# Gated MLP on one core: the last 48 turns by Strassen's algorithm, partial sums added in DRAM by DMA

## The chip, the cores and the metric

One core of a Trainium2 chip runs the whole program. Its engines are TensorE (PE, with its weight loads as PEld), VectorE (DVE), ScalarE (ACT), GpSimd (POOL) and SyncE (SP), which issues the DMAs. A time is the device time of one execution in microseconds (us); the measure is the median of several runs.

## The reference, cut to what matters

```python
attn_out = _attn_ref(q, k, v, lam)            # linear attention with decay: (4, 8, 768, 64)
x = attn_out.transpose(0, 2, 1, 3).reshape(3072, 512)
x = _moe_ref(x, phi, w1, w2)                  # soft mixture of 8 experts, 32 slots: (3072, 512)

def _moe2_ref(x, w_in, w_out):                # the gated MLP: d_model 512, d_ff 2048
    h = x @ w_in
    g = h * (1.0 / (1.0 + np.exp(-1.702 * h)))
    return g @ w_out                          # out (3072, 512)
```

w_in and w_out come as 64-bit floats and are turned into 32-bit ones on the chip. The mixture ends as x = c @ slot_out with only 32 slots, so the kernel forms slot_out @ w_in once (`W2s`) and gets h as W2s times c. What remains large is g @ w_out: 3072 x 2048 x 512.

## The kernel before

Attention, slots and experts fill the first 195 us, and neither version differs there in what it computes. Then the gated MLP runs in **turns**. Tokens are cut into 4 groups `tg` of TG = 768, and d_ff into 16 blocks `f` of 128; a turn is one pair (tg, f), and `order` lists all 64.

A turn j does two things on TensorE. It makes h for turn j + 2 (`h_mm`, L940: two matmuls of 384 columns), and it adds block f into the output of its 768 tokens (`out_mm`, L987): for each of 6 token tiles of 128 rows, three matmuls of 512 columns, ghi x whi, ghi x wlo and glo x whi, since operands are split into a high and a low part of the type fp32r. The six sums stand in six PSUM banks `ob`. ScalarE applies the gelu (`h_gate`, L948) and rounds g to the high part (`h_hi`, L951); VectorE takes the low part as the difference (`h_lo`, L954).

The first three token groups are interleaved, so that the conversion of w_in and w_out (`conversion`, L185 to L195, VectorE; `convert_abs`, L176, ScalarE) can keep up. The tables `LATE_IN` and `LATE_OUT` say at which turn each piece is converted, `load_late` brings its 64-bit form into one of NST = 3 buffers `f64` on SP's queue, and `split_w` splits w_out into `whi` and `wlo`. A token group that is left half done has its sums copied to SBUF (`part`, L994) and added at its end (L998). The program is written in a fixed order by hand (`tc.manual_schedule()`): each engine executes its instructions in the order of the code, `do_out` places other work between the matmuls of a turn by their number (`at`, `extra`), and semaphores carry the dependences. PSUM has eight banks, named in `BANKS`.

The last two turns run together, and the very last token tile is done in two halves of 256 columns (`out_last`, L1015), so that the first half is stored under the second.

Of the kernel before, what the change touches and what calls it, by code (L numbers as in the profile page):

```python
# [17 lines left out]
def attention_moe_gelu_kernel(  # L18
# [32 lines left out]
    NE = 1  # L51
# [6 lines left out]
    NHG = 2  # L58

    LATE_IN = {1: (2, 4, 5, 6), 2: (7, 8, 9, 10), 3: (11, 12, 13, 14)}  # L60
    LATE_OUT = {4: 6, 5: 10, 6: 12, 7: 14}
# [101 lines left out]
    w_in_sb = {n: winp.tile([P, KD, 512], F32, name=f"w_in{n}") for n in range(NE)}  # L163

    def load_f64(key, src, pool, n, bufs):
        t = pool.tile([P, n, 2], U32, tag="f64", name="f64", bufs=bufs)
        SP.dma_start(out=t.rearrange("p n t -> p (n t)"), in_=src)
        staged[key] = t
# [306 lines left out]
    with tc.manual_schedule():  # L475
# [296 lines left out]
        def convert_early(f):  # L772
            convert_abs(("out", f))
            wo[f] = ex.tile([P, DM], F32, tag="wo", name="wo", bufs=3)
            return conversion(("out", f), wo[f], DVE)
# [12 lines left out]
        for e in range(E):  # L788
# [7 lines left out]
            if e == 4:  # L796

                slotc_cm.__exit__(None, None, None)
                slotb_cm.__exit__(None, None, None)
                ex_cm = tc.tile_pool(name="ex", bufs=1, side="left", reuse_waits="tile")  # L800
                ex = ex_cm.__enter__()
                whi, wlo = [ex.tile([P, DM], F32R, name="whi0")], [ex.tile([P, DM], F32R, name="wlo0")]
            if e == E - 2:
                split_c(E - 1)
# [4 lines left out]
        order = [(tg, f) for tg in range(NHG) for f in range(HF)] + [(NHG, f) for f in range(NF)]  # L809
        order += [(tg, f) for tg in range(NHG) for f in range(HF, NF)]  # L810
        order += [(tg, f) for tg in range(NHG + 1, NT // TG) for f in range(NF)]
        first_of = {f: min(order.index((tg, f)) for tg in range(NHG + 1)) for f in range(NF)}
# [12 lines left out]
        def load_late():  # L825
# [7 lines left out]
            load_f64(key, src, ex, DM, NST)  # L833
# [12 lines left out]
        soT = w2p.tile([P, KD, G, NS], F32, name="soT")  # L846
        W2s = w2p.tile([P, DFF], F32R, name="W2s")
        wp = [w2p.tile([P, 512], F32R, name=f"wp{j}") for j in range(2)]
        w2raw = w2p.tile([P, 512], F32, name="w2raw")
        isumr = tailp.tile([P, P], F32R, tag="xT", name="isumr", bufs=NHP + 1)  # L850
        POOL.tensor_copy(out=isumr, in_=isum4.rearrange("p g s -> p (g s)"))
        for n in w_late:
            w_in_sb[n] = w_in_sb[n - 2] if n > 1 else mp.tile([P, KD, 512], F32, name=f"w_in{n}")

        def convert_late(j, rounds=9):
            work = []
            for key in turns.get(j, ()):
                if key[0] == "out":
                    o = wo[key[1]] = ex.tile([P, DM], F32, tag="wo", name="wo", bufs=3)
# [31 lines left out]
        load_late()  # L891
# [40 lines left out]
        bh, g, ghi, glo = {}, {}, {}, {}  # L932

        def h_mm(j, us=(0, 1)):
# [8 lines left out]
            g[j] = mp.tile([P, TG], F32, tag="g", name="g", bufs=2)  # L943
            ghi[j] = mp.tile([P, TG], F32R, tag="ghi", name="ghi", bufs=3)
            glo[j] = mp.tile([P, TG], F32R, tag="glo", name="glo", bufs=3)
# [34 lines left out]
        def out_mm(j, t, i):  # L980
            tg, f = order[j]
            begin = j == 0 or order[j - 1] != (tg, f - 1)
            end = j == NJ - 1 or order[j + 1] != (tg, f + 1) or (t == NTT - 1 and j == NJ - LAST - 1)
# [7 lines left out]
            if f < NF - 1:  # L991

                part[tg, t] = mp.tile([P, DM], F32, tag=f"part{t}" if tg in (0, NTG - 1) else f"part{tg}_{t}", name="part")
                ACT.activation(out=part[tg, t], in_=ob[t], func=AF.Copy)  # L994
                return
            o = mp.tile([P, DM], F32, tag="o", name="o", bufs=3)
            if (tg, t) in part:
                DVE.tensor_tensor(out=o, in0=ob[t], in1=part[tg, t], op=ALU.add)  # L998
            elif t % 2 == 0:
# [4 lines left out]

        def out_last():

            t = NTT - 1
            r0 = (NTG - 1) * TG + t * P
            terms = [(jj, a[jj], w[order[jj][1]]) for jj in range(NJ - LAST, NJ)
                     for a, w in ((ghi, whi), (ghi, wlo), (glo, whi))]  # L1010
            o = mp.tile([P, DM], F32, tag="o", name="o", bufs=3)
            for u in range(2):
                b = bank(HB[u], "bo")
                for n, (jj, a, w) in enumerate(terms):
                    PE.matmul(b[:, :H2], a[:, t * P:(t + 1) * P], w[:, halves[u]], start=(n == 0), stop=(n == len(terms) - 1))  # L1015
                DVE.tensor_tensor(out=o[:, halves[u]], in0=b[:, :H2], in1=part[NTG - 1, t][:, halves[u]], op=ALU.add)
                SP.dma_start(out=out[r0:r0 + P, halves[u]], in_=o[:, halves[u]])

        def do_out(j, at):
# [4 lines left out]
            elif j == NJ - LAST:  # L1024

                seq = [(jj, t, i) for t in range(NTT - 1) for jj in range(j, NJ) for i in range(3)]
# [4 lines left out]
            if j == NJ - LAST:  # L1031
                out_last()
# [3 lines left out]
        def w2_rest():  # L1036
# [7 lines left out]
                 (11, 4): lambda: w2_a(2, "xt"), (12, 4): lambda: w2_b(2, "xt"), (12, 8): lambda: w2_c(2),  # L1044
                 (15, 4): lambda: w2_a(3, "xt"), (16, 4): lambda: w2_b(3, "xt"), (16, 8): lambda: w2_c(3)}

        NJ = NTG * NF
        AHEAD = 2
        LAST = 2
# [6 lines left out]
        by_turns(second)  # L1056
        h_mm(0)
# [7 lines left out]
        for j in range(NJ - LAST + 1):  # L1065
            at = {n: work for (jj, n), work in extra.items() if jj == j}
            if j > 0:
                at[9] = lambda: ahead(j + AHEAD)
                if j in (9, 12, 16):

                    at[9], at[12] = lambda: h_mm(j + AHEAD, (1,)), at[9]
            do_out(j, at)

# [34 lines left out]
```

## Time and profile before

| | |
|---|---|
| median of 3 runs | 495.46 us (495.11 to 495.68) |
| span of the profiled execution | 493.7 us |
| PE, PEld busy | 485.0 us (98%), 380.7 us (77%) |
| DVE, ACT, POOL busy | 276.1, 273.9, 62.4 us |
| output matmuls of L987 | 382 of each of three kinds, 449 us busy in sum |
| DMA, HBM | 69.28 MB read, 6.29 MB written |

The span goes from the first to the last instruction of the profiled execution; the run's own time has some 1.8 us around it (495.46 against 493.7). A matmul's listed duration holds its passage through the array, so matmuls overlap one another: what one costs is read from the distance of starts. Of other engines too the distance of starts can be shorter than the duration.

### The profile page before, as it was taken

To read this page: it belongs to the slowest core of one execution; us is meant where nothing else is said; L and a number is where in the kernel's file an instruction comes from. 1 tells how busy PE (TensorE), PEld (TensorE's weight loads), DVE (VectorE), ACT (ScalarE), POOL (GpSimd) and SP (SyncE) were. 2 spreads that over 40 slices of the span, in tenths; PEclk is the share of its full clock that TensorE was granted. 3 is DMA by queue.
4 is the path that set the end of the run, shared out by engine and by line. 5 is a ranking of instruction groups with operands and counts; after the bars stand their busy time and mean duration, and the time that the engine had idled before them with its cause. 6 is when DMAs were issued, how large, how long until landed. Compare 5 with 4: busy or idle time off the path is not lost.

```text
span 493.7 us, 9458 instructions
## 1 busy us (share of the span) xinstructions
PE 485.0 (98%) x3561; PEld 380.7 (77%) x3561; DVE 276.1 (56%) x616; ACT 273.9 (55%) x569; POOL 62.4 (13%) x109
## 2 busy tenths in 40 slices
PE   8999999999999999999999999999999999999997
PEld 5887877877876445787877888888888888888886
DVE  4867888988874114997999884312251223322112
ACT  5778677777853335786876755533443344334432
POOL 3544344442212000000000000000000000000000
PEclk9999999999999999999999999999999999999999
DMA  8999999999999996344344310300030001100003
GB/s 183 259 285 291 277 267 286 282 265 276 238 348 355 381 394 252 116 139 160 129 170 142 116 44 0 127 1 0 1 127 1 0 1 66 64 1 0 1 0 127
DMA packets 82860, 76.18 MB, mean 154 GB/s; under 512 B 54400, under 2 KB 62848, under 8 KB 82816
## 3 DMA queue, kind: packets, MB, share of 16 engines
q1 hardware_dynamic: 82672, 75.58, 49.1%
q8 instruction: 28, 0.46, 0.4%
q14 instruction: 16, 0.13, 0.1%
q10 hardware_dynamic: 144, 0.00, 0.0%
HBM read 69.28 MB, written 6.29 MB: 153 GB/s over the span
## 4 chain that ended last, share of the span: by engine, by line
PE 85%; DVE 6%; DMA 6%; ACT 1%; issue 1%; SPq 1%; DVEq 0%
PE bo L987 52%; PE bhh L940 4%; PE bs L293 4%; PE bacc L765 3%; PE bh L743 3%; PE bx L340 3%; DMA stage<-in_moe_w_in_dram 3%; PE bx L332 2%; PE bq L255 2%; PE bst L306 2%; PE bt L351 1%; DMA w<-in_moe_w_dram 1%; PE bk L257 1%; DVE AT L296 1%; DMA v<-in_v_dram 1%
## 5 line engine op out<-in xcount | busy, mean ns | idle before, releaser
L987 PE MATMUL bo<-whi,glo 128*128 128x512 f32 x382 | 149.9, 394 | 0.0
L987 PE MATMUL bo<-wlo,ghi 128*128 128x512 f32 x382 | 149.8, 393 | 0.1
L987 PE MATMUL bo<-whi,ghi 128*128 128x512 f32 x382 | 149.0, 392 | 0.1
L954 DVE TENSOR_TENSOR glo<-g,ghi 128x768 fp32r<-128x768 f32 x64 | 61.3, 957 | 134.6 <-ACT ghi L951 134.4
L948 ACT ACTIVATE g<-bhh 128x384 f32<-128x384 f32 x128 | 56.3, 489 | 125.7 <-PE bhh L940 122.7
L987 PEld LDWEIGHTS bo<-wlo,ghi 128*128 128x128 f32 x382 | 71.7, 188 | 16.6 <-issue 2.5
L987 PEld LDWEIGHTS bo<-whi,glo 128*128 128x128 f32 x382 | 71.7, 188 | 15.7 <-DVE glo L954 0.3
L987 PEld LDWEIGHTS bo<-whi,ghi 128*128 128x128 f32 x382 | 71.7, 188 | 14.3 <-DVE W2s L898 0.5
L951 ACT ACTIVATE ghi<-g 128x768 fp32r<-128x768 f32 (+1 forms) x65 | 54.3, 836 | 2.1
L274 POOL TENSOR_TENSOR qdT<-qT,qtab 128x384 f32<-128x384 f32 x32 | 32.1, 1002 | 39.5 <-PE bx L332 17.8
L293 PEld LDWEIGHTS bs<-qT,kT 64*128 64x128 f32 x384 | 26.5, 191 | 13.1 <-DVE zsum L453 4.2
L293 PE MATMUL bs<-qT,kT 64*128 64x128 f32 x384 | 33.3, 295 | 1.8 <-DVE AT L296 1.3
L296 DVE TENSOR_TENSOR AT<-bs,dec 128x384 f32<-128x384 f32 x64 | 32.5, 550 | 3.0 <-PE bs L293 2.2
L940 PE MATMUL bhh<-cT,W2s 128*128 128x384 f32 x128 | 33.4, 337 | 0.0
L265 ACT ACTIVATE qT<-bq 128x384 f32<-128x384 f32 x32 | 22.6, 705 | 16.4 <-PE bq L255 15.4
L940 PEld LDWEIGHTS bhh<-cT,W2s 128*128 128x128 f32 x128 | 23.9, 188 | 5.5
L281 ACT ACTIVATE kd<-k,dec 128x192 f32<-128x192 f32 x64 | 25.5, 447 | 2.9 <-DVE dec L497 1.3
L340 PE MATMUL bx<-AT,v 128*64 128x128 f32 x384 | 27.0, 273 | 0.0
L340 PEld LDWEIGHTS bx<-AT,v 128*64 128x64 f32 x384 | 21.0, 137 | 0.1
L332 PE MATMUL bx<-qdT,sa 128*128 128x128 f32 x128 | 19.8, 277 | 0.0
L317 DVE SCALAR_TENSOR_TENSOR sa<-sa,qtab,bst 64x64 f32<-64x64 f32 x64 | 17.9, 280 | 2.1
L306 PE MATMUL bst<-v,kd 128*64 128x64 f32 x320 | 17.6, 232 | 1.4 <-DMA v<-in_v_dram 1.2
(171 smaller groups left out, 597.9 us busy)
## 6 DMA issues: line engine op xcount, KB each, us to landing
w<-in_moe_w_dram SPq DMA_DIRECT2D x64, 512.0 KB, 6.3
f<-in_moe_w_out_dram SPq DMA_DIRECT2D x15, 512.0 KB, 3.2
qr<-in_q_dram SPq DMA_DIRECT2D x32, 192.0 KB, 4.2
k<-in_k_dram SPq DMA_DIRECT2D x64, 96.0 KB, 4.0
v<-in_v_dram SPq DMA_DIRECT2D x64, 96.0 KB, 4.0
f<-in_moe_w_in_dram SPq DMA_DIRECT2D x12, 512.0 KB, 4.1
out_dram<-o SPq DMA_DIRECT2D x23, 256.0 KB, 2.1
stage<-in_moe_w_in_dram SPq DMA_DIRECT2D x8, 256.0 KB, 4.1
```

Source lines behind the costliest of these rows:

```text
L274: POOL.tensor_tensor(out=qdT[s], in0=qT[s].rearrange("m (c i) -> m c i", c=R), in1=qtab[:, hp, None, :].to_broadcast([P, R, P]), op=ALU.mult)
L281: ACT.activation(out=t[:, :, h, :], in_=k_t[s][:, :, h, :], func=AF.Copy, scale=dec[:, 2 * hp + h, P - 1:P])
L293: PE.matmul(bs[h][:, cs], kT[s][hs, cs], qT[s][hs, cs], start=True, stop=True)
L296: DVE.tensor_tensor(out=t, in0=bs[h][:, :HS].rearrange("m (c i) -> m c i", c=R), in1=dec[:, 2 * hp + h, None, :].to_broadcast([P, R, P]), ...
L306: PE.matmul(bst[h * D:(h + 1) * D, c * D:(c + 1) * D], kd[s][:, c, h, :], v_t[s][:, c, h, :], start=True, stop=True)
L332: PE.matmul(bx[:, c * P:(c + 1) * P], state(s, first + c), qdT[s][:, c, :], start=(c == chunks[0]), stop=False)
L340: PE.matmul(bx[h * D:(h + 1) * D, c * P:(c + 1) * P], v_t[s][:, c, h, :], AT[s, h][:, c, :], start=False, stop=(c == R - 1))
L940: PE.matmul(bh[j][u][:, :HS], W2s[:, f * P:(f + 1) * P], cT[tg // (NTG // 2)][:, t0:t0 + HS], start=True, stop=True)
L948: ACT.activation(out=g[j][:, u * HS:(u + 1) * HS], in_=bh[j][u][:, :HS], func=AF.Gelu_apprx_sigmoid)
L951: ACT.activation(out=ghi[j][:, o], in_=g[j][:, o], func=AF.Copy)
L954: DVE.tensor_tensor(out=glo[j][:, o], in0=g[j][:, o], in1=ghi[j][:, o].bitcast(F32), op=ALU.subtract)
L987: PE.matmul(ob[t], a[j][:, t * P:(t + 1) * P], w[f], start=(begin and i == 0), stop=(end and i == 2))
```

## The change

The 64 turns become 32 as before and 48 of a new kind. The old kind now covers f = 0 to 3 of token groups 0 and 1, f = 0 to 7 of group 3, and all of group 2; the tables of conversions are spread to match, and the partial sums of groups 0, 1 and 3 are stored to `out` in DRAM instead of being kept in SBUF.

The rest (groups 0 and 1 from f = 4, group 3 from f = 8) is done in **groups** of 256 tokens (gi, nine of them; six turns in each of the first six, four in the last three). A new turn takes a pair p of blocks f = 2p, 2p + 1: a product of a 2 x 2 matrix of 128 x 128 blocks of g with a 2 x 2 matrix of 128 x 256 blocks of w_out. Strassen's algorithm (in Winograd's form) needs 7 block products instead of 8, each here three matmuls of 256 columns. For that it wants sums of blocks: four of w_out per pair (`make_sums`, `make_his`, `make_lows`, made once in the first half), and four of g per turn (in `s_h`, VectorE), with high and low parts of all seven (`s_hi`, ScalarE; `s_lo`, VectorE). h of turn j + 3 is made in turn j (`s_h`: two matmuls of 256). The sums of a group stand in 3 PSUM banks, alternating between two sets, and the first product in a shared one.

At a group's end `ev_m` (ScalarE) and `ev_a` to `ev_d` (VectorE) combine the seven sums to the four blocks of the output in `cells`, during the first three turns of the next group, and two DMAs on POOL's queue add them to `out` in DRAM. The last group is added on chip: its partial sums are loaded (`load_before`), and its last two turns run together (`last_turns`).

```diff
+    PAIR_AT = {2: 18, 3: 21, 4: 24, 5: 26, 6: 28, 7: 29}
+    LAST_HF = 8
...
+        WHOLE = 2
+        SPLIT = [tg for tg in range(NT // TG) if tg != WHOLE]
+        done = {tg: LAST_HF if tg == SPLIT[-1] else HF for tg in SPLIT}
+        order = [(tg, f) for tg in SPLIT for f in range(done[tg])] + [(WHOLE, f) for f in range(NF)]
...
-                part[tg, t] = mp.tile([P, DM], F32, tag=f"part{t}" if tg in (0, NTG - 1) else f"part{tg}_{t}", name="part")
-                ACT.activation(out=part[tg, t], in_=ob[t], func=AF.Copy)
+            o = mp.tile([P, DM], F32, tag="o", name="o", bufs=3)
+            if tg != WHOLE:
+                ACT.activation(out=o, in_=ob[t], func=AF.Copy)
+                SP.dma_start(out=out[r0:r0 + P, :], in_=o)
                 return
...
+            for o, x, y in ((b11, b12, b11), (b12, b22, b12), (b22, b22, b11), (b21, b21, b22)):
+                DVE.tensor_tensor(out=o, in0=x, in1=y, op=ALU.subtract)
...
+        PRODS = {1: (0, 1), 2: (2, 2), 3: (6, 3), 4: (1, 7), 5: (3, 4), 6: (4, 5), 7: (5, 6)}
+        PO = (2, 6, 7, 5, 3, 4, 1)
...
+        def s_h(j):
...
+            for k in range(2):
+                PE.matmul(b[:, k * NC:(k + 1) * NC], W2s[:, (2 * p + k) * P:(2 * p + k + 1) * P],
+                          cT[tg // 2][:, t0:t0 + NC], start=True, stop=True)
+            a = gs(j)
+            ACT.activation(out=a[:, :2 * NC], in_=b, func=AF.Gelu_apprx_sigmoid)
+            a21, a11, a22, a12, s1, s2, s3, s4 = (a[:, i * P:(i + 1) * P] for i in range(8))
+            for o, x, y, op in ((s1, a21, a22, ALU.add), (s3, a11, a21, ALU.subtract),
+                                (s2, s1, a11, ALU.subtract), (s4, a12, s2, ALU.subtract)):
+                DVE.tensor_tensor(out=o, in0=x, in1=y, op=op)
...
+            ACT.activation(out=sh[j], in_=gs(j)[:, P:], func=AF.Copy)
...
+            DVE.tensor_tensor(out=sl[j], in0=gs(j)[:, P:], in1=sh[j].bitcast(F32), op=ALU.subtract)
...
+            PE.matmul(bank_of(gi, i)[1], x, w, start=begin, stop=end)
...
+        def ev_a(gi):
+            DVE.tensor_tensor(out=cells[:, U2:C11 + 1:C11 - U2], in0=cells[:, M1:M1 + 1].to_broadcast([P, 2, H1]),
+                              in1=two(sbank[gi][0]), op=ALU.add)
...
+        def ev_out(gi):
+            for k in range(2):
+                POOL.dma_start(out=rows_of(gi, k), in_=cells[:, C11 + 2 * k:C11 + 2 * k + 2], accum_op=ALU.add)
...
+            at = {0: [lambda: s_hi(j + 2)], 9: [lambda: s_h(j + 3), lambda: s_lo(j + 2)]}
+            if gi and k < len(EV):
+                at[14] = [lambda: EV[k](gi - 1)]
...
+            s_turn((NSJ - 2, NSJ - 1), {2: [lambda: EV[2](gi - 1)], 6: [lambda: ev_m(gi)], 18: [first], 30: [second], 42: [lambda: ev_d(gi)]},
+                   (1, 2, 6, 7, 5, 3, 4))
```

On TensorE, in the second half before: a piece of a turn around its h pair (`bo` an output bank, `bhh` the bank of h, numbers those of a block of w_out).

```order
L987 MATMUL bo<-whi_3324,ghi 128x512
L987 MATMUL bo<-wlo_3339,ghi 128x512
L987 MATMUL bo<-whi_3324,glo 128x512
L940 MATMUL bhh<-cT,W2s 128x384 x2
L987 MATMUL bo<-whi_3324,ghi 128x512
```

In the change, the same place of a new turn (`bp` a group's bank, `tc` sums of w_out, `bsh` the bank of h, `GHI` and `GLO` the parts of g and its sums).

```order
L1166 MATMUL bp<-whi_3326,GHI 128x256
L1166 MATMUL bp<-wlo_3341,GHI 128x256
L1166 MATMUL bp<-whi_3326,GLO 128x256
L1166 MATMUL bp<-tc,GHI 128x256 x2
L1166 MATMUL bp<-tc,GLO 128x256
L1166 MATMUL bp<-tc,GHI 128x256 x2
L1166 MATMUL bp<-tc,GLO 128x256
L1122 MATMUL bsh<-cT,W2s 128x256 x2
L1166 MATMUL bp<-tc,GHI 128x256 x2
L1166 MATMUL bp<-tc,GLO 128x256
```

The 512-column products became runs of 256, three per block product, and a pair of 256 stands where the pair of 384 stood.

On VectorE, the end of the program before: one low part per turn, and the copies and adds of finished tiles.

```order
L998 TENSOR_TENSOR o<-bo,part 128x512 x3
L954 TENSOR_TENSOR glo<-g,ghi 128x768 x14
L1002 COPY o<-bo 128x512 x2
L1016 TENSOR_TENSOR o<-bo,part 128x256 x2
L1103 UNCONDITIONAL_BRANCH
```

In the change, VectorE in the first three turns of a later group (`f` is the buffer that `cells` lies in).

```order
L1176 TENSOR_TENSOR f_3197<-f_3197,bp 128x2x256
L1129 TENSOR_TENSOR G_all<-G_all 128x128 x4
L1141 TENSOR_TENSOR GLO<-G_all,GHI 128x896
L1180 TENSOR_TENSOR f_3197<-f_3197,bp 128x256
L1183 TENSOR_TENSOR f_3197<-f_3197,bp 128x2x256
L1129 TENSOR_TENSOR G_all<-G_all 128x128 x4
L1141 TENSOR_TENSOR GLO<-G_all,GHI 128x896
L1187 TENSOR_TENSOR f_3197<-f_3197,bp 128x512
```

Each turn now has four sums and a wider low part, and `ev_a` (L1176), `ev_b` and `ev_c` (L1180, L1183) and `ev_d` (L1187) stand behind the low parts, ahead of the next turn's sums.

In the change, VectorE at the end of the program: the eviction of the group before the last, then that of the last with the loaded partial sums (`before`).

```order
L1180 TENSOR_TENSOR f_3197<-f_3197,bp 128x256
L1183 TENSOR_TENSOR f_3197<-f_3197,bp 128x2x256
L1187 TENSOR_TENSOR f_3197<-f_3197,bp 128x512
L1176 TENSOR_TENSOR f_3197<-f_3197,bp 128x2x256
L1232 TENSOR_TENSOR f_3197<-f_3197,before 128x256 x2
L1180 TENSOR_TENSOR f_3197<-f_3197,bp 128x256
L1232 TENSOR_TENSOR f_3197<-f_3197,before 128x256
L1183 TENSOR_TENSOR f_3197<-f_3197,bp 128x2x256
L1232 TENSOR_TENSOR f_3197<-f_3197,before 128x256
L1187 TENSOR_TENSOR f_3197<-f_3197,bp 128x512
```

Both evictions write the same cells; the DMAs that add the former group's cells in DRAM lie between its L1187 and the last group's L1176.

## Rows read from the trace of the kernel before

**Rows 1.** The page: busy time of engines, and granted TensorE clock by slice.

```profile
PE 485.0 (98%) x3561; PEld 380.7 (77%) x3561; DVE 276.1 (56%) x616; ACT 273.9 (55%) x569; POOL 62.4 (13%) x109
...
PEclk9999999999999999999999999999999999999999
```

**Rows 2.** The page: the chain that ended last, by engine and by line.

```profile
PE 85%; DVE 6%; DMA 6%; ACT 1%; issue 1%; SPq 1%; DVEq 0%
PE bo L987 52%; PE bhh L940 4%; PE bs L293 4%; PE bacc L765 3%; PE bh L743 3%; PE bx L340 3%; DMA stage<-in_moe_w_in_dram 3%; PE bx L332 2%; PE bq L255 2%; PE bst L306 2%; PE bt L351 1%; DMA w<-in_moe_w_dram 1%; PE bk L257 1%; DVE AT L296 1%; DMA v<-in_v_dram 1%
```

**Rows 3.** Windows: length; busy of PE, PEld, DVE, ACT, POOL; clock; DMA; GB/s.

```profile
255.00:300.00 45.00, 45.00 (x204) 36.37 (x203) 41.13 (x67) 30.19 (x55) 0.00 (x0) 1.00 0.27 94
300.00:350.00 50.00, 50.00 (x225) 41.60 (x224) 13.13 (x16) 21.07 (x38) 0.00 (x0) 1.00 0.09 32
```

**Rows 4.** Waits from 300 to 478 us: us in total, times, longest.

```profile
DVE glo L954 <- ACT ghi L951: 128.5, 40, 3.6
ACT g L948 <- PE bhh L940: 102.2, 38, 2.8
```

**Rows 5.** Timeline of PE: start and duration in us, line, tiles.

```profile
347.56 0.39 PE L987 MATMUL bo<-whi,ghi 128*128 128x512 f32 x1
...
349.61 0.51 PE L940 MATMUL bhh<-cT,W2s 128*128 128x384 f32 x2
...
479.81 0.51 PE L940 MATMUL bhh<-cT,W2s 128*128 128x384 f32 x2
```

**Rows 6.** The chain in order of time, one turn: start, us, what.

```profile
475.84 4.14 PE bo L987 x18
```

**Rows 7.** Timeline of all engines at the end of the program.

```profile
482.25 0.39 PE L987 MATMUL bo<-whi,ghi 128*128 128x512 f32 x1
...
488.82 0.39 PE L987 MATMUL bo<-whi,glo 128*128 128x512 f32 x1
...
489.05 0.28 PE L1015 MATMUL bo<-whi,ghi 128*128 128x256 f32 x1
489.05 0.19 PEld L1015 LDWEIGHTS bo<-wlo,ghi 128*128 128x128 f32 x1
...
489.25 0.60 ACT L1000 ACTIVATE o<-bo 128x512 f32<-128x512 f32 x1 [2.12 <-PE bo L987]
...
490.36 0.28 PE L1015 MATMUL bo<-whi,glo 128*128 128x256 f32 x1
...
490.68 0.42 DVE L1016 TENSOR_TENSOR o<-bo,part 128x256 f32<-128x256 f32 x1 [0.23 <-PE bo L1015]
```

**Rows 8.** Timeline of DVE and ACT where VectorE has a queue of work.

```profile
281.48 0.69 DVE L781 TENSOR_TENSOR wlo<-wo,whi 128x512 fp32r<-128x512 f32 x1
282.08 0.68 DVE L195 SCALAR_TENSOR_TENSOR wo<-cvm,wo 128x512 f32<-128x512 f32 x1
282.68 0.42 DVE L185 TENSOR_SCALAR wo<-f 128x512 uint32<-128x512 uint32 x1
283.14 0.69 DVE L188 SCALAR_TENSOR_TENSOR wo<-f,wo 128x512 uint32<-128x512 uint32 x1
...
284.48 0.95 DVE L954 TENSOR_TENSOR glo<-g,ghi 128x768 fp32r<-128x768 f32 x1
285.35 0.68 DVE L781 TENSOR_TENSOR wlo<-wo,whi 128x512 fp32r<-128x512 f32 x1
...
288.07 0.85 ACT L951 ACTIVATE ghi<-g 128x768 fp32r<-128x768 f32 x1
288.82 0.62 ACT L778 ACTIVATE whi<-wo 128x512 fp32r<-128x512 f32 x1
```

**Rows 9.** Groups by line and shape, xcount, busy us, mean ns of one.

```profile
L1000 ACT ACTIVATE o<-bo 128x512 f32<-128x512 f32 x6 | 3.6, 598 | 7.0 <-PE bo L987 7.0
...
L505 DVE TENSOR_TENSOR qtab<-qtab 128x128 f32<-128x128 f32 x1 | 0.3, 291 | 0.0
```

**Rows 10.** DMA issues: tiles, queue, count, KB each, median us to landing.

```profile
out_dram<-o SPq DMA_DIRECT2D x23, 256.0 KB, 2.1
stage<-in_moe_w_in_dram SPq DMA_DIRECT2D x8, 256.0 KB, 4.1
...
out_dram<-o SPq DMA_DIRECT2D x2, 128.0 KB, 1.8
```

## What the change should do to the time

> **What bounds the kernel now.** I read the busy times first: TensorE works for 485.0 of 493.7 us at full clock, VectorE and ScalarE for 56% and 55% [rows 1]. The clock that was granted is the upper of its two levels, 2.4 GHz, in every slice [rows 1]. The chain that ended last is 85% TensorE, 52% the output product of line 987 alone [rows 2]. The average hides that VectorE is busy for 41.1 us of the 45 between 255 and 300 us, where w_in and w_out are converted, and for 13.1 of the next 50 [rows 3]. From 300 us on, the longest waits are VectorE's for ScalarE and ScalarE's for TensorE [rows 4]; TensorE itself is busy without a gap [rows 3]. So a product taken out of the last stage shortens the kernel, until something else is late.
>
> A turn is 18 output products of 512 columns and two h products of 384. The h pairs start at 349.61 and 479.81 us, 29 turns apart: 4.49 us a turn [rows 5]. The 33rd turn begins at 347.56 us [rows 5] and the last matmul ends at 490.36 + 0.28 = 490.64 us [rows 7]. The half that is replaced takes 143.1 us on TensorE.
>
> **The new TensorE work.** 48 turns of 7 x 3 = 21 products of 256 columns, and 45 x 2 h products of 256 (three turns' h is made before): 1008 + 90 = 1098 matmuls. Columns fall by an eighth, but each matmul is half as long, so what one costs beside its columns decides. The trace holds this very form: the twelve matmuls of line 1015 start 489.05 to 490.36 us, 1.31/11 = **0.119 us** each, every one with its own weight load and with ScalarE at work beside five of them [rows 7]. Two of 256 thus cost 0.238, against one of 512 at (488.82 - 482.25)/29 = 0.2266 in the quiet stretch [rows 7] and 4.14/18 = 0.230 in a usual turn [rows 6]: 3.5 to 5% dearer for the same columns. Since a 512 is 0.004 slower in a usual turn than in the quiet stretch, I take **0.120**; bounds 0.119 and 0.124 (the whole surcharge on the shorter form). 1098 x 0.120 = 131.8 us, for 143.1: **11.3 us** less; 12.4 and 7.0 at the bounds. A new turn is 23 x 0.120 = 2.76 us.
>
> **Is VectorE fast enough?** Two operations that don't depend on each other start 0.60 us apart at 512 elements and 0.87 at 768 (281.48, 282.08; 284.48, 285.35), though one lasts 0.69 or 0.95; a dependent one starts 0.03 to 0.04 after its source ends (282.68 + 0.42, then 283.14) [rows 8]. Scaled, a follow-on costs 0.20 at 128, 0.33 at 256 and 1.00 at 896 elements. The four sums of a turn: s1, s3, s2 at 0, 0.20, 0.40, and s4 after s2 (0.29 long [rows 9], with the gap 0.33) at 0.73; the engine is free at 0.93, s4 done at 1.02. The low parts: 1.00. So **1.93 us of 2.76** per turn. A group's eviction adds 0.60, 0.46 + 0.60 and 0.60 in three turns: 2.53, 2.99, 2.53. Only the second is longer than a turn, by 0.23, and it is paid back in the next. Six-turn groups need 13.8 of 16.6 us, four-turn groups 10.0 of 11.0.
>
> ScalarE: the high parts (896) 0.87 behind one another, by 0.75 at 768 (288.07, 288.82 [rows 8]) plus 128 elements at the same rate; the gelu of 512 from PSUM 0.60, as its copy [rows 9]; 1.47 of 2.76. The loop through both engines (sums 1.02, high parts 0.87, the next gelu 0.60, three hand-overs of 0.03) is 2.6 us, under a turn. Deadline: in turn j the gelu of j+3 ends about 2.1 us in (9 products, the h pair, 0.2, 0.60), the sums hold VectorE until 3.05, and the low parts of j+2 end near 4.1; TensorE wants them at its third matmul of turn j+2, 5.76 us in. **1.6 us to spare**, so an eviction's 0.23 is hidden. If that cover goes, the cost is in the second rival.
>
> **The first 32 turns.** Conversions come one a turn instead of up to two, and are spread to turn 26: 2.25 us (0.34 + 0.60 x 3 and dependency gaps), low parts of g 0.87, of w_out 0.60: 3.7 of 4.49. The pair sums and low parts of T add 1.7 and 1.6 us in turns 18 to 30; the worst run, turns 18 to 20 (5.5, 5.4, 4.7), leaves VectorE 2.1 us behind, against the two turns by which h runs ahead. I cost it at nothing. The 18 new partial stores on SP stand behind load_late's slot waits; a bank is wanted only 3.8 us after its tile is copied, and a store lands in 2.1 [rows 10]: nothing. The hand-over to the new turns: the sixth high and low parts are made in turn 31, the banks were copied before; nothing.
>
> **The added sums in DRAM.** POOL issues two adding DMAs per group, 16 in all; no trace of before has one, nor any DMA on POOL's queue. Their duration X is the unknown. They read `cells`, which ev_a of the next group overwrites, so VectorE's queue, with the sums and low parts behind ev_a, waits for them. From below X is a plain store of 256 KB, 2.1 us; from above a 256 KB load at its 4.1 beside other traffic and then a store, 6.2 [rows 10]. An add makes a read trip and a write trip, so I take two stores: **4.2**. Between the add of one group and ev_a of the next lie two turns in the four-turn groups, less ev_d: 4.8 us, and 1.6 of slack behind it: no stall up to X = 6.4; in six-turn groups eleven or more.
>
> The Trainium skill, page "DMA: Bandwidth & Descriptors", section "Anatomy of one DMA — SWDGE (gpsimd) path", gives about 2.0 us plus the bytes over 436 GB/s, an estimate of 2.6 us for 256 KB on this queue, and names no term for adding. By it the end would come 1.6 us sooner, 487.6. No run here shows it.
>
> **The end.** Here X is bare. The merged last two turns start at 347.56 + 1056 x 0.120 = 474.3 us and TensorE ends at 479.5. VectorE's ev_d of group 7 ends about 1.5 into them, 475.8 (low parts of the last turn 1.4 to 2.4 of the turn before, then ev_b, ev_c, ev_d). The add is issued, and ev_a of the last group must wait until 475.85 + 4.2 = 480.1. Then VectorE's chain: ev_a 0.72, two adds 0.36 + 0.36, ev_b 0.46, add 0.46, ev_c 0.60, add 0.46, ev_d 0.69: 4.1, by the widths above, to 484.2. Two stores of 256 KB behind it: before, the last VectorE row ends at 491.10 and the span at 493.7, 2.6 [rows 7]; here 0.33 more to issue the second and 0.3 for the larger size (2.1 for 1.8 [rows 10]): 3.2, so 487.4. Before, 3.0 us lay between TensorE's end and the span's; now **7.9**. The tail gives back 4.9 of the 11.3.
>
> Sum: span 493.7 - 11.3 + 4.9 = 487.3, and the rounded steps above give 487.4. The median of the runs, 495.46, is 1.8 above the profiled span; so **489.2 us**. Bounds: X = 2.1 and 0.119 give 486.0; X = 6.2 and 0.124 give 495.6.
>
> **Rivals.** *VectorE becomes the bound.* If short operations don't overlap as the wide ones do (none of 128 elements in a chain stands in the trace), each costs its own time and gap: 4 x 0.32 + 1.12 = 2.4 a turn, and 2.6 per eviction: 17.0 for a six-turn group (16.6 on TensorE), 12.2 for a four-turn one (11.0). Five times 0.4 and three times 1.2, less the slack of 1.6: 4.0 us, 493.2. Against it stand the starts 0.60 apart of operations 0.69 long [rows 8]. *Slower: the adding DMA is long.* From X = 6.4 VectorE stands at ev_a of groups 6 and 7, TensorE runs dry behind it, and the tail grows too: (X - 4.2) + 2 (X - 6.4). At X = 9 that is 10.0: 499.2. It turns the sign at X near 8. For it: no row shows the operation, and POOL must issue two in a row. Against: both plain trips together are 6.2 at their slowest. *Weight loads become the bound.* A load lasts 0.19 us [rows 7], longer than a 256 matmul's slot; were loads to run one after another, 1098 x 0.188 is 206 us, 74.6 more: 563.8. Against it stand twelve in a row at 0.119 [rows 7]. The Trainium skill, page "TensorE: Matmul & The Clock Gate", section "The mechanism" of its Part 3, has a load overlap with a running matmul only where the row groups differ. Here all 128 rows are used each time and loads still start with the matmul before them; the trace disagrees with that rule. *The reordered first half stalls*, by 2 to 3 us where VectorE is behind: 491.7.
>
> **How the numbers follow.** Forecast 0.72, VectorE 0.12, long add 0.07, stalls in the first half 0.08, loads 0.01. The range, 485.8 to 494.5, holds the forecast without its dearest corner, the VectorE case and the stalls. Faster by over 0.2% (what a measurement of this kernel can tell from none): 0.87, with small parts of all but two cases lost to the rest; within 0.2% 0.05; slower 0.08.
>
> **What would show it.** Right: L1166 matmuls of 256 starting 0.12 us apart, 2.76 us from h pair to h pair, no TensorE wait for GLO, and VectorE idle before ev_a of the last group for a DMA. Wrong: TensorE waiting for L1141 in the turns with an eviction (VectorE), a long wait of L1176 in groups 7 and 8 (the add), matmuls spaced above 0.125, or TensorE gaps before 347 us.

## The result: 490.1 us, and the profile after

The changed kernel takes **490.1 us** (median of four runs, 487.86 to 492.1); the kernel before took 495.57 (median of four, 495.11 to 496.54). The ratio is 0.9881, 95% interval 0.9850 to 0.9913: 1.2% faster. The prediction said 489.2, with 485.8 to 494.5 as its range.

The page of the changed kernel, the lines that answer to [rows 1, 2]:

```profile
PE 471.3 (96%) x4019; PEld 391.2 (80%) x4019; DVE 369.8 (76%) x895; ACT 302.6 (62%) x605; POOL 77.7 (16%) x125
...
PEclk9999999999999999999999999999999999999997
...
PE 81%; DVE 9%; DMA 7%; ACT 2%; issue 1%; POOL 0%; DVEq 0%; ACTq 0%
```

TensorE works for 13.7 us less, and VectorE for 94 us more. The granted clock is the upper level, 2.4 GHz, as before; only in the last slice, in which TensorE's work ends (at 478.91 us), is it lower. The chain gave 4% from TensorE to VectorE and DMA: that is the tail.

Busy time by window (columns as in [rows 3]), from the first half of the gated MLP into the new turns:

```profile
300.00:350.00 50.00, 50.00 (x234) 41.92 (x233) 43.24 (x89) 32.96 (x67) 0.00 (x0) 1.00 0.11 39
350.00:400.00 50.00, 50.00 (x423) 50.00 (x422) 41.15 (x103) 28.57 (x40) 3.71 (x4) 1.00 0.24 47
```

TensorE has no gap in either. In the new turns weight loads fill the whole window, and 423 matmuls stand in 50 us where before 225 stood. The waits from 360 to 470 us, the longest (us in total, times, longest):

```profile
POOL out_dram L1196 <- DVE G_all L1129: 272.7, 7, 190.6
ACT GHI L1136 <- DVE G_all L1129: 40.4, 33, 1.4
DVE G_all L1129 <- ACT G_all L1125: 12.6, 19, 0.7
ACT f L1173 <- PE bp L1166: 6.3, 8, 0.8
```

VectorE and ScalarE now wait mostly for each other. ScalarE's waits for TensorE, 63.0 us in the same stretch of the kernel before, have shrunk to 6.3. TensorE does not appear as one that waits.

The timeline of TensorE: the first product of the new turns, the first h pair, and the last product.

```profile
348.26 0.28 PE L1166 MATMUL bp<-whi,GHI 128*128 128x256 f32 x1
...
349.32 0.40 PE L1122 MATMUL bsh<-cT,W2s 128*128 128x256 f32 x2
...
478.63 0.28 PE L1166 MATMUL bp<-tc,GLO 128*128 128x256 f32 x1
```

VectorE's timeline at the end (idle before and its releaser in brackets), and behind it POOL's and SP's:

```profile
475.29 0.69 DVE L1187 TENSOR_TENSOR f<-f,bp 128x512 f32<-128x512 f32 x1
480.48 0.69 DVE L1176 TENSOR_TENSOR f<-f,bp 128x512 f32<-128x512 f32 x1 [4.50 <-DMA out_dram<-f]
...
482.33 0.42 DVE L1232 TENSOR_TENSOR f<-f,before 128x256 f32<-128x256 f32 x1
...
483.91 0.69 DVE L1187 TENSOR_TENSOR f<-f,bp 128x512 f32<-128x512 f32 x1
...
476.28 1.76 POOL L1196 DMA_DIRECT2D out_dram<-f  x2 [6.21 <-DVE f L1187]
...
484.63 0.82 SPq L1253 DMA_DIRECT2D out_dram<-f  x2
```

`ev_d` of the group before the last ends at 475.98, POOL issues its two adding DMAs, and `ev_a` of the last group stands until 480.48 for them. It writes over cells that only the first of the two reads: that one lands 4.1 us after its issue, at 480.4. The second is issued at 476.82 and lands 5.4 us later, at 482.2, 0.1 us ahead of the sum that overwrites its cells (L1232, 482.33). TensorE had ended at 478.63 + 0.28 = 478.91.

**Where the time went.** Every run also differs in how long the stage ahead of the gated MLP takes: its first matmul of the MLP (`bwarm`) starts between 189.6 and 193.6 us in the profiles of this study, 191.67 before and 192.52 after. So I split the span at that point:

| stretch, us | before | after | difference |
|---|---|---|---|
| start to `bwarm` | 191.67 | 192.52 | +0.85 |
| to the start of the new turns (33rd turn before) | 155.89 | 155.74 | -0.15 |
| to TensorE's end | 143.08 | 130.65 | -12.43 |
| to the span's end | 3.06 | 9.59 | +6.53 |
| span | 493.7 | 488.5 | -5.2 |

Without the first row the change is worth some 6 us: 12.4 gained on TensorE and half of it given back behind it.

### The profile page after: what moved, and what is told of

It reads as the page before. It is cut to its first block, busy times and chain, and to the rows that moved or that the text cites. A ratio compares the mean times of both kernels' runs of the same rounds, so it can differ in the third digit from the quotient of the medians.

```text
span 488.5 us, 10721 instructions
## 1 busy us (share of the span) xinstructions
PE 471.3 (96%) x4019; PEld 391.2 (80%) x4019; DVE 369.8 (76%) x895; ACT 302.6 (62%) x605; POOL 77.7 (16%) x125
## 4 chain that ended last, share of the span: by engine, by line
PE 81%; DVE 9%; DMA 7%; ACT 2%; issue 1%; POOL 0%; DVEq 0%; ACTq 0%
PE bo L1000 26%; PE bp L1166 22%; PE bs L297 4%; PE bacc L769 3%; DMA stage<-in_moe_w_in_dram 3%; PE bh L747 3%; PE bx L344 3%; PE bx L336 3%; PE bsh L1122 2%; PE bhh L953 2%; PE bq L259 2%; PE bst L310 2%; PE bt L355 2%; DVE AT L300 1%; PE bk L261 1%; PE bp L437 1%
## 5 line engine op out<-in xcount | busy, mean ns | idle before, releaser
L1000 PE MATMUL bo<-wlo,GHI 128*128 128x512 f32 x192 | 75.3, 395 | 0.1
L1000 PE MATMUL bo<-whi,GLO 128*128 128x512 f32 x192 | 75.1, 394 | 0.0
L1000 PE MATMUL bo<-whi,GHI 128*128 128x512 f32 x192 | 74.8, 393 | 0.1
L1136 ACT ACTIVATE GHI<-G_all 128x896 fp32r<-128x896 f32 x48 | 45.8, 954 | 45.8 <-DVE G_all L1129 45.7
L1129 DVE TENSOR_TENSOR G_all<-G_all 128x128 f32<-128x128 f32 x192 | 47.4, 288 | 19.8 <-ACT G_all L1125 17.3
L1166 PE MATMUL bp<-tc,GHI 128*128 128x256 f32 x288 | 55.8, 282 | 0.0
L1141 DVE TENSOR_TENSOR GLO<-G_all,GHI 128x896 fp32r<-128x896 f32 x48 | 52.1, 1084 | 0.0
L1166 PE MATMUL bp<-whi,GHI 128*128 128x256 f32 x192 | 49.5, 281 | 0.0
L1166 PE MATMUL bp<-wlo,GHI 128*128 128x256 f32 x192 | 49.2, 282 | 0.0
L1166 PE MATMUL bp<-whi,GLO 128*128 128x256 f32 x168 | 47.6, 283 | 0.0
```

The costliest lines, as they stand in the source:

```text
L1000: PE.matmul(ob[t], a[j][:, t * P:(t + 1) * P], w[f], start=(begin and i == 0), stop=(end and i == 2))
L1129: DVE.tensor_tensor(out=o, in0=x, in1=y, op=op)
L1136: ACT.activation(out=sh[j], in_=gs(j)[:, P:], func=AF.Copy)
L1141: DVE.tensor_tensor(out=sl[j], in0=gs(j)[:, P:], in1=sh[j].bitcast(F32), op=ALU.subtract)
L1166: PE.matmul(bank_of(gi, i)[1], x, w, start=begin, stop=end)
```

## The experiments

Three questions: is it TensorE that sets the new turn, and with how much room; what does the adding DMA cost and save; and is the tail the wait for it? Below, "from `bwarm`" is the span less the start of `bwarm`, which takes the front's spread out; the changed kernel has 296.0, the kernel before 302.0. The changed kernel itself ran again beside the first experiments:

> The changed kernel as it is, beside which the other runs of this call stand on the same chip. Theory: TensorE sets the pace of the new turns, 2.73 us each (23 matmuls 0.119 us apart), and the tail after its last matmul is 9 to 10 us long, of which VectorE waits 4.5 for the DMA that adds group 7's sums. Time 488 to 492. Rival: the spread of the four runs (487.9 to 492.1) comes from that DMA; then a second profile shows another tail by as much as its time differs.

Measured: 491.12 us (489.39 to 492.25), span 489.5, from `bwarm` 296.1. Beside it stand the runs below.

### Cells of their own for the last group

```diff
-        cells = f64[:, :2, :].rearrange(...)
+        cells = f64.rearrange(...)
             def first():
+                nonlocal C11, C12, C21, C22
+                C11, C12, C21, C22 = range(8, 12)
                 ev_a(gi)
```

> The last group's four output blocks get cells of their own (the third, free buffer of f64), so that nothing waits for the adding DMA at the end. Theory (the end waits for the DMA): VectorE's ev_a of the last group follows ev_d of group 7 at once, the chain of 4.1 us ends about 4.4 us sooner, 485.6. Rival (VectorE's own chain or the last matmul holds the end anyway): gain under 1 us, 489 or more.

Measured: **484.43 us** (483.32 to 487.75), ratio to before 0.9782 (0.9741 to 0.9823), 6.7 under the changed kernel by medians; from `bwarm` 292.3, which is 3.8 less. The same three rows of VectorE and SP, in this kernel:

```profile
476.39 0.69 DVE L1187 TENSOR_TENSOR f<-f,bp 128x512 f32<-128x512 f32 x1
...
477.27 0.69 DVE L1176 TENSOR_TENSOR f<-f,bp 128x512 f32<-128x512 f32 x1 [0.19 <-PE bp L1166]
...
481.42 0.82 SPq L1255 DMA_DIRECT2D out_dram<-f  x2
```

The wait of 4.50 us for the DMA is one of 0.19 for TensorE. The tail behind TensorE's end is 485.9 - 480.0 = 5.9 instead of 9.6. So 3.7 of the 6.5 us that the tail gave back were the wait for the adding DMA, and nothing but a buffer took them.

### Plain stores in the place of adding ones

```diff
-                POOL.dma_start(out=..., in_=..., accum_op=ALU.add)
+                POOL.dma_start(out=..., in_=...)
```

> The 16 DMAs on POOL's queue store instead of adding; the output lacks the partial sums in the rows of eight groups. Theory (an add makes a read trip and a write trip): issue to release falls from 4.2 us to 2.1 to 2.8, the end comes 1.4 to 2.1 us sooner, 488 to 488.7, and nothing changes before the last two turns. Rival (POOL's issuing of 1.1 us a piece makes the length, not the adding): landing stays at 4 us and more, gain under 0.5 us.

Measured: 489.41 us (486.67 to 490.92), from `bwarm` 294.2, 1.9 less than the changed kernel. The issue rows (count, KB each, median us to landing) of the changed kernel and then of this one:

```profile
out_dram<-f POOLq DMA_DIRECT2D x16, 256.0 KB, 5.3
```

```profile
out_dram<-f POOLq DMA_DIRECT2D x16, 256.0 KB, 2.6
```

and `ev_a` of the last group, with the issue that it waits for:

```profile
478.28 0.69 DVE L1176 TENSOR_TENSOR f<-f,bp 128x512 f32<-128x512 f32 x1 [2.72 <-DMA out_dram<-f]
...
475.86 1.07 POOL L1196 DMA_DIRECT2D out_dram<-f  x2 [6.90 <-DVE f L1187]
```

These medians mix two kinds: of each pair, the first add lands after 3.9 to 4.2 us (once 5.6) and the second after 5.2 to 6.4; the plain stores of most pairs land after 2.3 and 2.6 (up to 5.0 in two pairs). So adding nearly doubles the landing, and also POOL's time to issue one (0.87 and 1.22 us in most pairs, 0.54 here). From issue to release of the cells that `ev_a` writes it is 480.48 - 476.28 = 4.2 us for the add and 2.4 for the store.

### Fewer and more products per turn

```diff
             for n, o in enumerate(seq):
                 ...
+                if o[1] in (3, 5, 7) and o[2] == 1:
+                    continue
                 s_mm(*o)
```

> Three of the 21 product matmuls of each new turn are left out (the low part of the weights in products 3, 5 and 7), so TensorE needs 20 x 0.119 = 2.38 us a turn. If TensorE alone sets the pace: 17 us less, about 473. If the loop through VectorE and ScalarE (sums 1.02, high parts 0.87, gelu 0.60, hand-overs 0.1 to 0.2: 2.6 to 2.7) comes next: a turn of 2.6 to 2.7, 2 to 6 us less, 484 to 488. If VectorE were already co-bound by its busy time: under 1 us less.

Measured: 487.04 us (485.98 to 487.74), from `bwarm` 293.2: about 3 us less, of the 17 that TensorE's columns alone would give. VectorE's timeline here, through the end of an eviction:

```profile
400.06 1.03 DVE L1129 TENSOR_TENSOR G_all<-G_all 128x128 f32<-128x128 f32 x4
401.00 1.09 DVE L1141 TENSOR_TENSOR GLO<-G_all,GHI 128x896 fp32r<-128x896 f32 x1
402.00 0.42 DVE L1180 TENSOR_TENSOR f<-f,bp 128x256 f32<-128x256 f32 x1
402.45 0.69 DVE L1183 TENSOR_TENSOR f<-f,bp 128x512 f32<-128x512 f32 x1
403.05 1.01 DVE L1129 TENSOR_TENSOR G_all<-G_all 128x128 f32<-128x128 f32 x4
...
405.65 1.02 DVE L1129 TENSOR_TENSOR G_all<-G_all 128x128 f32<-128x128 f32 x4
...
408.26 1.02 DVE L1129 TENSOR_TENSOR G_all<-G_all 128x128 f32<-128x128 f32 x4 [0.58 <-ACT G_all L1125]
```

The sums of successive turns start 2.61 us apart, with 0.58 us in which VectorE waits for the gelu: this is the loop of sums, high parts and gelu, which the prediction put at 2.6. Around `ev_b` and `ev_c` the turn is 403.05 - 400.06 = 2.99, the prediction's 2.99. So TensorE's turn of 2.73 is longer than that loop by 0.12 us and no more.

```diff
                 s_mm(*o)
+                if o[1] in (2, 5, 3) and o[2] == 1:
+                    s_mm(*o)
```

> The changed kernel with three product matmuls more per new turn: the low part of the weights is multiplied a second time in products 2, 3 and 5, so that a turn has 24 product matmuls, as many as eight block products of three terms would have in this form (those three product sums are therefore not the reference's). VectorE, ScalarE and the DMAs do what they did. If the new half is bound by TensorE's columns: 48 x 3 x 0.119 = 17.1 us more than the changed kernel, 491 + 17 = 508 us, and h pair to h pair 2.73 + 0.36 = 3.09. If it is bound by the loop through VectorE and ScalarE (2.6 a turn) or by the weight loads, which these extra matmuls lengthen as well, the first gives less than 17 us, the second more; a loop that is only just hidden (0.12 us under the turn) should not show at all here.

Measured: 506.55 us (504.67 to 509.31), from `bwarm` 311.5: 15.4 more than the changed kernel either way. Its h pairs, on TensorE:

```profile
402.88 0.40 PE L1122 MATMUL bsh<-cT,W2s 128*128 128x256 f32 x2
...
405.96 0.40 PE L1122 MATMUL bsh<-cT,W2s 128*128 128x256 f32 x2
...
409.06 0.40 PE L1122 MATMUL bsh<-cT,W2s 128*128 128x256 f32 x2
```

3.08 and 3.10 us apart, as worked out: the new half is bound by TensorE's columns. The stretch of the products is 17.0 us longer, against the 17.1 expected; the tail is 1.6 shorter, since `ev_d` of the group before then ends further ahead of TensorE's end. This is also the price of doing eight block products in the new form: 506.55 would be 11 us slower than the kernel before. The saved eighth product is the whole gain, and it first pays for matmuls of half the length and for the tail.

### More work for VectorE, in the loop and beside it

```diff
             for o, x, y, op in ((s1, a21, a22, ALU.add), (s3, a11, a21, ALU.subtract),
+                                (s3, a11, a21, ALU.subtract), (s3, a11, a21, ALU.subtract),
```

> The changed kernel with two more 128x128 subtractions per turn among the sums of VectorE (they write a sum again that is there already), 0.2 us each, so 0.4 us inside the loop sums, high parts, gelu. By my account the loop lasts 2.6 us against TensorE's 2.73, so 0.27 us of 0.4 must show in every turn: 3.0 us from h pair to h pair, 48 x 0.27 = 13 us more, about 504 us. If the loop has more room than that (a rival: TensorE alone sets the turn, operands being made three turns ahead), nothing shows: 491 us.

Measured: 518.75 us (516.27 to 520.38), from `bwarm` 323.7. The mechanism holds, my price for it did not. The two extra operations wait for each other, so that they take 0.65 us, not 0.4 (1.68 us of sums where 1.02 stood):

```profile
425.69 1.68 DVE L1130 TENSOR_TENSOR G_all<-G_all 128x128 f32<-128x128 f32 x6 [0.58 <-ACT G_all L1125]
...
428.93 1.68 DVE L1130 TENSOR_TENSOR G_all<-G_all 128x128 f32<-128x128 f32 x6 [0.56 <-ACT G_all L1125]
```

Sums start 3.24 to 3.27 apart: 2.61 + 0.65. TensorE now waits for the low parts (41 waits of `bp` for line 1142, 13.2 us in the waits of 340 to 490 us). (3.26 - 2.73) x 47 is 25 us, and the eight turns with `ev_b` and `ev_c`, at 3.64, add 3.

```diff
             DVE.tensor_tensor(out=sl[j], in0=gs(j)[:, P:], in1=sh[j].bitcast(F32), op=ALU.subtract)
+            for _ in range(2):
+                DVE.tensor_tensor(out=sl[j][:, :P], in0=gs(j)[:, P:2 * P], in1=sh[j][:, :P].bitcast(F32), op=ALU.subtract)
```

> The same two subtractions of 128x128 per turn, 0.4 us of VectorE, but behind the low parts, where no gelu waits for them (a low part is written again). VectorE's work per turn rises from 1.93 to 2.33, 2.93 in the mean with the evictions' share, against 2.73: if only the loop counts, turns without an eviction do not grow and turns with one grow by at most 0.4; over the eight groups I expect 3 to 8 us more than the changed kernel (494 to 499), clearly less than where the same work stands in the loop (504). If it is VectorE's sum of work that sets the turn, both places cost the same.

Measured: 501.03 us (500.6 to 502.11), from `bwarm` 308.0: 11.9 more than the changed kernel (9.9 by medians), above my 3 to 8, for the same reason; these two also cost 0.65 (0.12 of gap and 0.54). The h pairs around an eviction:

```profile
386.32 0.40 PE L1122 MATMUL bsh<-cT,W2s 128*128 128x256 f32 x2
...
389.11 0.40 PE L1122 MATMUL bsh<-cT,W2s 128*128 128x256 f32 x2
...
392.74 0.40 PE L1122 MATMUL bsh<-cT,W2s 128*128 128x256 f32 x2
...
395.92 0.40 PE L1122 MATMUL bsh<-cT,W2s 128*128 128x256 f32 x2
```

At a cost of 0.65 the account closes: six turns of 1.94 + 0.65 and an eviction of 2.26 are 17.8 us of VectorE per group of six, and the h pairs above are 2.79, 3.63 and 3.18 apart with 2.74 between the rest, 17.8 in all, against 16.4. So beside the loop, VectorE's sum of work per group decides, and in the loop it is the loop. That the loop is dearer, 27.6 against 11.9, tells the two apart.

### The partial sums added on VectorE

```diff
-                POOL.dma_start(out=..., in_=..., accum_op=ALU.add)
+                POOL.dma_start(out=..., in_=...)
-            if gi == len(groups) - 1 and k == 1:
-                at[2] = [load_before]
+            if k == 1:
+                at[2] = [lambda: load_before(gi)]
-        EV = (lambda gi: ev_a(gi), lambda gi: (ev_b(gi), ev_c(gi)), ...
+        EV = (lambda gi: first_of(gi), lambda gi: second_of(gi), ...
```

`first_of` and `second_of` are what `first` and `second` do for the last group: `ev_a` and two adds, `ev_b`, an add, `ev_c`, an add.

> The adding DMAs undone: in all nine groups the partial sums are loaded into SBUF (two loads of 256 KB on SP's queue, as the last group has them already) and added on VectorE with four more operations of 256 columns; POOL then stores plainly, as in the run with plain stores (489.4 us), which is the kernel to compare with. The adds cost VectorE 0.8 us in each of a group's first two turns after the last: 1.94 + 1.40 = 3.3 us and 1.94 + 1.85 = 3.8 us against TensorE's 2.73. Two theories. The prediction's: operands have 1.6 us to spare, and that hides the 1.65 of excess in the six-turn groups; only the four-turn ones lose, 0.65 each: 490 to 491.5. The one that the runs before suggest: VectorE and ScalarE catch up only by 0.1 us a turn and have about 0.4 us in hand, so 1.2 us is lost in each of eight groups: 9 to 10 us, 498 to 499.

Measured: **498.08 us** (ten runs, 497.44 to 498.91), ratio to before 1.0036 (1.0015 to 1.0057): slower than the kernel before. From `bwarm` 304.2, 10.0 over the run with plain stores. The second theory's size is right, and the trace shows why. VectorE's timeline from the last of a group's quiet turns through an eviction:

```profile
402.18 1.02 DVE L1129 TENSOR_TENSOR G_all<-G_all 128x128 f32<-128x128 f32 x4 [0.56 <-ACT G_all L1125]
...
404.12 0.68 DVE L1176 TENSOR_TENSOR f<-f,bp 128x512 f32<-128x512 f32 x1
404.83 0.76 DVE L1246 TENSOR_TENSOR f<-f,before 128x256 f32<-128x256 f32 x2
405.51 1.01 DVE L1129 TENSOR_TENSOR G_all<-G_all 128x128 f32<-128x128 f32 x4
...
409.30 1.01 DVE L1129 TENSOR_TENSOR G_all<-G_all 128x128 f32<-128x128 f32 x4
...
411.90 1.02 DVE L1129 TENSOR_TENSOR G_all<-G_all 128x128 f32<-128x128 f32 x4
...
414.51 1.02 DVE L1129 TENSOR_TENSOR G_all<-G_all 128x128 f32<-128x128 f32 x4 [0.58 <-ACT G_all L1125]
```

The two loaded turns take 3.33 and 3.79 us, and every other 2.60 or 2.61, the loop's pace, although VectorE idles 0.58 in most of them: it is behind all the time and catches up at 2.73 - 2.61 = 0.12 a turn. A group of six loses 0.60 + 1.06 (3.33 and 3.79 against 2.73) and recovers four times 0.12, so 1.2 us is lost in each, and TensorE waits (waits from 340 to 490 us):

```profile
PEld bp L1166 <- DVE GLO L1141: 8.3, 9, 1.9
PE bp L1166 <- DVE GLO L1141: 6.5, 7, 1.7
```

The 1.6 us that the prediction had "to spare" are there, once: the h pairs around the first eviction, a lag of 1.66, lengthen by some 0.2 us, those of each later one by 0.06 and 1.06. It is a stock that the loop hardly refills. "0.4 us in hand", as I had put it, is what four turns put back.

So adding by DMA is worth 304.2 - 296.1 = 8.1 us here, tail included, more than the 6.0 that the whole change gains: with the sums added on VectorE nothing of the seven products would be left.

### Can the rest of the tail go?

```diff
             def first():
                 (as in cells of their own)
                 add(cells[:, C11], cells[:, C11], o1[:, 0])
+                store(0, 0, C11, SP)
             ...
                 ev_c(gi, slice(C12, C22 + 1, C22 - C12))
+                store(1, 1, C22, SP)
             ...
-            for k in range(2):
-                SP.dma_start(out=rows_of(gi, k), in_=...)
+            for h, (c, x, queue) in enumerate(((C12, U4, SP), (C21, U3, ACT))):
+                add(cells[:, c], cells[:, x], two(sbank[gi][1])[:, h])
+                store(h, 1 - h, c, queue)
```

> The changed kernel with the last group's four output blocks in cells of their own (so that nothing of the last tail waits for the adding DMA), each of the two diagonal blocks stored as soon as it is summed, the last sum cut in two of 256 columns, and the last two stores issued from two queues. Cells of their own alone gave 484.4. The last sum of 0.69 ends for one block 0.3 us earlier, stores of 128 KB instead of 256 KB land 0.2 to 0.5 us earlier: 482.5 to 484.5, most likely 483.3. If the landing does not depend on the size, 484.1.

Measured: 486.31 us (485.77 to 489.09), from `bwarm` 292.3, the same as with cells of their own alone. A miss: the stores of 128 KB land in 3.5 and 3.6 us, where those of 256 KB landed in 2.2 in the changed kernel. There the adds had landed by then. With cells of their own alone the two last stores, one behind the other on SP's queue and beside the adds, took 2.8:

```profile
out_dram<-f SPq DMA_DIRECT2D x2, 256.0 KB, 2.8
```

Then the kernel with cells of their own once more, and with the two last stores issued from two queues:

```diff
-            for k in range(2):
-                SP.dma_start(out=rows_of(gi, k), in_=...)
+            for k, queue in enumerate((SP, ACT)):
+                queue.dma_start(out=rows_of(gi, k), in_=...)
```

> The kernel with cells of their own for the last group once more, with more rounds, since single runs spread by 4 us: 484.4 was its median; the same within 1 us, 483.5 to 485.5.

> Cells of their own, and the last two stores issued from two queues (SP's and ScalarE's) instead of one behind the other on SP's: the second store starts 0.4 us sooner, so 0.4 us less than the run beside it, 484.0. If the end is set by the adding DMAs of the group before, which are still under way then (they were issued 4 us ahead of the last store and take 5), it is the same as beside it.

Measured: 485.73 (483.78 to 486.2; ratio 0.9782, 0.9755 to 0.9808) and 486.89 us (484.01 to 487.67; 0.9804, 0.9775 to 0.9833); from `bwarm` 292.4 and 292.6. The second queue brings nothing. Its issue rows, with the adds of the group before still under way:

```profile
out_dram<-f POOLq DMA_DIRECT2D x16, 256.0 KB, 5.2
...
out_dram<-f SPq DMA_DIRECT2D x1, 256.0 KB, 3.4
out_dram<-f ACTq DMA_DIRECT2D x1, 256.0 KB, 3.6
```

Is it the adds that slow them?

```diff
 (on the kernel with two queues)
-                POOL.dma_start(out=..., in_=..., accum_op=ALU.add)
+                POOL.dma_start(out=..., in_=...)
```

> Cells of their own and two queues for the last stores, and POOL's DMAs store plainly instead of adding (so the partial sums are left out of the output of eight groups, and an add costs one trip less). No wait on the chip's engines depends on these DMAs any more. If the two last stores land late (3.4 and 3.6 us, against 2.2 in the changed kernel) because the adding DMAs of the group before are still under way beside them, they land in 2.2 to 2.5 here and the stretch from the end of the last sum to the end of the span falls from 4.8 to 3.7: about 485.0 for a kernel whose median was 486.9, or 482.2 - 1.1 = 481.1 of span at the same start. If two queues that store at once are slow by themselves, 4.8 stays.

Measured: 485.57 us (484.6 to 487.71), from `bwarm` 291.7. The same rows here:

```profile
out_dram<-f POOLq DMA_DIRECT2D x16, 256.0 KB, 2.6
...
out_dram<-f SPq DMA_DIRECT2D x1, 256.0 KB, 2.5
out_dram<-f ACTq DMA_DIRECT2D x1, 256.0 KB, 2.7
```

From the end of the last sum to the span's end it is 484.7 - 480.74 = 4.0 us, against 482.2 - 477.38 = 4.8 with the adds. So most of what the stores lost, 0.9 of 1.3 us of landing, is the company of the adds; the other 0.4 (2.6 against 2.2) stays where two queues store at once without adds. With the wait gone, the adds still cost something at the end, and neither smaller pieces nor a second queue gets round them.

## Why the prediction was right, point by point

- **TensorE (right, 1.1 too little).** 1098 matmuls of 256 start from 348.26 to 478.63, 130.37/1097 = 0.1188 us apart. I had chosen 0.120 between 0.119 and 0.124; the surcharge of a usual turn, seen on the 512s, is not there on the 256s. The stretch is 130.65 instead of 131.8, and the h pairs are 2.72 to 2.75 apart for 2.76.
- **VectorE (right).** The sums hold it for 0.94, the low parts for 1.00 us (predicted 0.93 and 1.00): in the steady turns below, sums start 2.72 apart, low parts 0.94 behind them, and 0.69 to 0.70 of each turn is idle. Short operations follow on as the wide ones of [rows 8] do, and the rival built on the contrary fell.

```profile
429.63 1.02 DVE L1129 TENSOR_TENSOR G_all<-G_all 128x128 f32<-128x128 f32 x4 [0.69 <-ACT G_all L1125]
430.57 1.08 DVE L1141 TENSOR_TENSOR GLO<-G_all,GHI 128x896 fp32r<-128x896 f32 x1
432.35 1.02 DVE L1129 TENSOR_TENSOR G_all<-G_all 128x128 f32<-128x128 f32 x4 [0.70 <-ACT G_all L1125]
```

- **The loop of 2.6 us (right),** 2.61 where TensorE doesn't hide it. What the prediction left out is that so thin a lead also sets how fast a lag is paid back. For this kernel it did not matter: the eviction's excess of 0.23 is two turns' worth of the lead.
- **The first 32 turns (right):** -0.15 us for "nothing", and within 0.05 of it in every kernel of this study (155.72 to 155.76 from `bwarm` to the first new product). The rival of a stalling first half fell.
- **The adding DMA (right, 0.25 too little, and the size in part by luck).** 4.2 us from issue to release, the "two stores" of the prediction; with the hand-over to POOL, 4.5 from `ev_d` to `ev_a`. But this is the first add of the pair. The prediction did not tell the two apart; the second takes 5.2 to 6.4 us, and no more is lost because its cells are wanted 1.8 us after those that `ev_a` writes. In the repeated run that was just too soon: at the same sum (L1232) VectorE stood for 0.24 us, until the second add had landed. In the groups before the last no wait but one of 0.22 us, in the repeated run, is put down to an add: `ev_c` in the group before the last, for a second add too. The Trainium skill's page "DMA: Bandwidth & Descriptors", section "Anatomy of one DMA — SWDGE (gpsimd) path", comes to an estimate of 2.6 us for 256 KB; the plain stores of the experiment land in 2.6 in the median, so the trace agrees there, and the add, which that section does not price, takes 5.3 in the median.
- **The end (right mechanism, 1.7 too little).** 9.6 us behind TensorE for the predicted 7.9. `ev_d` of the group before ends 2.9 us ahead of TensorE's end, not 3.7, because I placed the low parts of the last turn too early: +0.8. The add: +0.25. The chain of sums: 4.12 for 4.1. The stores: 3.9 for 3.2, the term that was mis-sized most in proportion. They are issued at once (484.63 and 485.02) and land in 2.2 us in the median, near the 2.1 of [rows 10]; the second lands at 487.3, 2.7 us behind the last sum, where before it was 1.7. Another 1.2 us then pass to the end of the span, 0.8 before; no engine computes in them. The trace has six waits of SP for semaphores there, some 0.06 us each, where before it has one, and then a closing sequence of all engines.
- **The front (not in the prediction):** +0.85 us in the profile.

The errors, -1.1, -0.15, +1.7 and +0.85, add up, but for rounding, to the 1.2 by which the profiled run, 490.36 us, is above 489.2. That the sum came so near is in part luck: what TensorE gained beyond the forecast stands against what the end cost beyond it. The weight-load rival fell with the first point. The Trainium skill's page "TensorE: Matmul & The Clock Gate", section "The mechanism" of its Part 3, would, by its rule that loads overlap running matmuls only where the row groups differ, have these loads wait (it also lets a load into the background weight buffer go ahead, which the prediction left out). Here, too, the trace disagrees with the rule on row groups: loads of 0.19 us each, all of 128 rows, beside matmuls that start 0.119 apart.

## What to carry to other kernels

Price the end of a program apart from its turns: half of what the cheaper product brought went into a tail that the profile before did not have, and more than half of that was one reused buffer. A slack of operands counts once; what an engine can pay back per turn is the difference between the turn and the loop that feeds it, here 0.12 us, and that number decides how much more work a helper engine takes. Where the helper has none to give, a DMA that adds in memory does the work for an engine that was idle, as long as nobody waits for its buffer.

## What the runs showed of the hardware

- A DMA that adds in DRAM, 256 KB on POOL's queue, lands 5.3 us after its issue in the median (3.9 to 6.4), a plain store on the same queue after 2.6 (2.3 to 5.0). Of two adds issued one behind the other the first mostly takes 3.9 to 4.2 and the second 5.2 to 6.4; why they differ stays open. Issuing an add holds POOL for 0.87 or 1.22 us in most pairs, issuing a plain store for 0.54. Plain stores of 256 KB on two other queues beside two adds land in 3.4 and 3.6 instead of 2.5 and 2.7, and two on one queue in 2.8 instead of 2.2.
- Two 128 x 128 operations on VectorE that follow each other on the same output cost 0.65 us together, where independent ones start 0.20 apart. I had priced them at 0.4, and both expectations that rested on it were too low.
- The stage ahead of the gated MLP, in which the DMA engines are busy nearly throughout (the page has 9 tenths or more in fourteen of the first sixteen slices), ends between 189.6 and 193.6 us in the profiled runs of this study. From there to the end, kernels with the same rows agree to 0.2 us. So the time of a single run can't show a difference of 2 us here, and the stretch behind that stage can; what causes the spread stays open.
